# The first feed-forward pair's down projection with tokens on the partitions, and its result turned by VectorE's 32x32 transposes

## The chip, the core and the metric

The kernel runs on one core of a Trainium2 chip. The metric is the device time of one execution in microseconds; before the change it is 1059.04 us, the median of three runs (1058.98 to 1059.52). On the core, TensorE multiplies matrices, VectorE, ScalarE and GpSimd do the elementwise work, and SP (SyncE) issues most of the DMAs. Each engine works through its own list of instructions in order.

## The reference

Attention with a block-causal mask over four batches of eight heads (576 positions, head size 64) gives 2304 tokens of 512 numbers. Two feed-forward pairs follow, each 512 to 2048 to 512, with different activations. All is float32.

```python
scores = scale * np.matmul(q, k.transpose(0, 1, 3, 2))
scores = np.where(block_i >= block_j, scores, -1e9)     # blocks of 64 positions
attn = softmax(scores)
x = (attn @ v).transpose(0, 2, 1, 3).reshape(2304, 512)
h = x @ moe_w_in                                        # first pair
y = np.maximum(0.01 * h, h) @ moe_w_out
h = y @ moe2_w_in                                       # second pair
g = np.where(h >= 1, h, np.where(h <= -1, 0, (h + 1) ** 2 / 4))
out = g @ moe2_w_out
```

## The kernel before

**Precision.** TensorE multiplies float32r, so most operands are split in a high and a low part, and a product is three matmuls: high by high, high by low, low by high. The names end in h and l: xh, xl; gh, gl; yh, yl; a weight's two parts lie in one tile (w1i, w1o, w2i, w2o). `three` (L536) is that triple.

**Stages.** The tokens go through the first pair in nine blocks j of 256, and the 2048 inner features in sixteen slices f of 128. `up1(j, f)` makes h with the features on the partitions (twelve matmuls), ScalarE makes g of it (L542), and g is split in gh and gl. `down1(j, f)` adds the slice's part of y: w1o stationary, g moving, 256 columns at a time, four groups e of 128 output features with three matmuls each. So y comes out with the output features on the partitions, two groups e in one PSUM bank, and two banks hold the four groups of a block. After f = 15, VectorE and ScalarE copy the four groups to SBUF (ysb, L575) and SP writes them to a DRAM tensor, ydram (L576). Between `up1(j, f)` and `down1(j, f)` stand one other `up1` in blocks 0 to 5 and three from block 6 on.

**Around it.** The attention of batch 0 comes first, beside the conversion of the first pair's weights; the heads of batches 1 to 3 are laid between the `up1` and `down1` of blocks 0 to 5. Batches 2 and 3 turn their probabilities by VectorE's 32x32 transposes (L316), DMAs to a DRAM tensor z (L321, pieces of 128 bytes) and DMAs back (pT, L341). One h bank serves `up1` while attention goes on. In blocks 6 and 7 the second pair's weights are staged through DRAM (L148, L151), in block 8 they are loaded (w, L155) and split (w2i, w2o). `load_y` reads ydram back as yh and yl, 512 tokens at a time. The second pair (`up2`, `down2`, from 650 us on) multiplies hh out of w2i and y, does cl, sq, gg, ggh, ggl on VectorE and ScalarE, and has g stationary and w2o moving with 512 columns: the tokens come out on the partitions.

**The order.** Up to block 5, `arrange` (L812) plans the order of each engine's list by a list schedule with prices from `span` (L761). From block 6 on the framework orders by the order in which the code was written and by what is free. Tiles of one tag share a ring of slots; a new tile waits until the slot's last reader is done. The g, gh and gl tiles come from the pool `two` up to block 5 (three slots each) and from the pool `bp` after (two, three and three). The second pair's pool `gp` (cl, sq, gg and so on) lies where the first pair's `two` and `one` pools lay.

Of the kernel before, what the change touches and what calls it, by code (L numbers as in the profile page):

```python
# [9 lines left out]
F32 = mybir.dt.float32  # L10
# [40 lines left out]
def attention_moe_moe(ctx: ExitStack, tc: tile.TileContext, qkv, w1, w2, out, B, H, S, D):  # L51
    nc = tc.nc
    NT, DM = out.shape
# [23 lines left out]

    ident = const.tile([P, P], F32, name="ident")
    make_identity(nc, ident)
    ydram = dram.tile([P, KC, NT], F32, name="ydram")  # L80
    wdram = dram.tile([KF, P, 1024], F32, name="wdram")

    def psum(tag, name):
# [474 lines left out]

    def down1(j, f):
        if f == 0:  # L560
            for e in range(0, KC, 2):
                y = psum("y", f"y{j}_{e}")
                for k in range(2):
                    yt[e + k] = y[:, k * NB:(k + 1) * NB]
        g = gt.pop((j, f))
        for e in range(KC):
            es = slice(e * P, (e + 1) * P)

            start, stop = f == 0 and e % 2 == 0, f == KF - 1 and e % 2 == 1
            wh, wl = W[1, "o", f]  # L570
            three(yt[e], wh[:, es], wl[:, es], *g, start, stop)
        if f == KF - 1:
            for e in range(KC):
                ysb = two_p.tile([P, 320], F32, tag="sc", name=f"ysb{j}_{e}", bufs=C["sc"])[:, :NB]
                copy(nc, pick("yevE", e), ysb, yt[e])  # L575
                nc.sync.dma_start(ydram[:, e, j * NB:(j + 1) * NB], ysb)  # L576

    blocks = [(t0, min(512, NT - t0)) for t0 in range(0, NT, 512)]
    ys = {}
# [1 line left out]
    def load_y(j):  # L581
        t0, n = blocks[j]
        y32 = yp.tile([P, KC, 512], F32, tag="y32", name=f"y32_{j}", bufs=1)
        nc.sync.dma_start(y32[:, :, :n], ydram[:, :, t0:t0 + n])
# [71 lines left out]
    for j in range(NBLK):  # L656
        final = j == NBLK - 1
        due_now(j)
        if j == due[-1]:
            arrange(tc)  # L660
            actx.close()
            gpool = (ctx.enter_context(tc.tile_pool(name="bp", bufs=2, reuse_waits="tile")), C["gB"], C["ghB"])
            sctx = ExitStack()
            sg = sctx.enter_context(tc.tile_pool(name="sg", bufs=C["sg"], reuse_waits="tile"))
        if final:
# [95 lines left out]
def span(ins, e, outs, srcs):  # L761
# [12 lines left out]
    w = max(n(x) for x in outs[:1] + srcs[:1]) if outs else 1  # L774
    if op == "DMACopy":
        kb = outs[0][2][0][1] * n(outs[0]) / 256
        small, spread = (x[0][0].name.startswith("z") for x in (outs, srcs))
        return 1350 + kb * 4.8 + 600 * spread, 520, kb * (7.6 if small else 6 if spread else 3.3)
    if e == "PE":
        if srcs[0][3] == F32 and not ins.is_transpose:  # L780
            return w / 0.6 + 165, w / 0.6 + 95, 0
        step = w / 2.4 + (17 if w >= 512 else 13)
        wide = n(srcs[1]) > 64 and w < 256 and not ins.is_transpose
# [219 lines left out]
```

## Time and profile before

| | |
|---|---|
| median of three runs | 1059.04 us |
| the profiled execution's own time | 1055.33 us |
| its span, first to last instruction | 1053.4 us |
| TensorE busy | 1009.1 us (96%) |
| VectorE busy | 716.8 us (68%) |
| ScalarE busy | 466.1 us (44%) |
| GpSimd busy | 226.4 us (21%) |
| granted TensorE clock, mean | 0.992 of full speed |

A share is a mean over the whole span and hides that stages have different limits, so the table by stretch of time is the one to read. A matmul's shown duration is longer than its pitch, since matmuls are pipelined: the pitch is read from the starts, or from a count of them over a stretch without a gap. What is after the arrow in a row (`<-ACT g L542`) is the instruction whose end let a waiting one go. SP's rows are issues of DMAs; how long a DMA takes to land is another row.

### The profile page before, as it was taken

How to read it: one execution, taken by the hardware profiler on the slowest of the kernel's cores; microseconds unless marked ns; L12 is line 12 of the kernel's file. 1: busy time of each engine (PE TensorE's matmuls, PEld its weight loads, DVE VectorE, ACT ScalarE, POOL GpSimd, SP SyncE). 2: the span in 40 equal slices, each digit the busy share in tenths (PEclk: the TensorE clock that was granted, in tenths of full speed). 3: DMA queues.
4: the chain of work that ended last, by engine and by line, in shares of the span. 5: the costliest groups of instructions: out<-in, count | busy, mean ns of one | idle time of the engine just before them, and what ended most of it. 6: DMA issues, size and time to landing. Idle time of an engine off the chain costs nothing. (4 is left out here: it accounts for less than half of the span.)

```text
span 1053.4 us, 18317 instructions
## 1 busy us (share of the span) xinstructions
PE 1009.1 (96%) x6382; PEld 896.7 (85%) x6382; DVE 716.8 (68%) x1866; ACT 466.1 (44%) x1163; POOL 226.4 (21%) x297
## 2 busy tenths in 40 slices
PE   8899889999999999898999899999999999999998
PEld 6568879998998989898999898888888888888887
DVE  7999999997888878887687778435333533433343
ACT  5676557684655545544444321223322422322233
POOL 4552022252332544534010145000000000000000
PEclk9999999999999999999999899999999999999999
DMA  9655112226677766665788765000100100000010
GB/s 351 218 161 176 45 53 73 59 68 145 146 160 160 153 156 135 148 148 114 236 291 292 239 232 177 1 1 15 66 1 1 60 1 0 20 21 1 1 40 21
DMA packets 161292, 115.50 MB, mean 110 GB/s; under 512 B 110768, under 2 KB 134320, under 8 KB 161200
## 3 DMA queue, kind: packets, MB, share of 16 engines
q1 hardware_dynamic: 158608, 109.62, 36.7%
q10 hardware_dynamic: 2592, 4.72, 1.2%
q8 instruction: 50, 0.82, 0.3%
q14 instruction: 42, 0.34, 0.1%
HBM read 83.62 MB, written 30.67 MB: 109 GB/s over the span
## 5 line engine op out<-in xcount | busy, mean ns | idle before, releaser
L537 PE MATMUL h<-xh,w1i 128*128 128x256 f32 x576 | 168.3, 292 | 14.9 <-ACT g L542 11.3
L538 PE MATMUL h<-xl,w1i 128*128 128x256 f32 x576 | 165.5, 288 | 4.7 <-DVE xl L38 4.2
L538 PE MATMUL y<-gl,w1o 128*128 128x256 f32 x576 | 163.9, 287 | 4.8 <-DVE gl L38 4.3
L539 PE MATMUL h<-xh,w1i 128*128 128x256 f32 x576 | 164.6, 286 | 0.0
L537 PE MATMUL y<-gh,w1o 128*128 128x256 f32 x576 | 160.6, 287 | 1.9 <-DVE gh L32 1.4
L539 PE MATMUL y<-gh,w1o 128*128 128x256 f32 x576 | 162.2, 284 | 0.0
L716 ACT ACTIVATE sq<-cl,half 128x512 f32<-128x512 f32 (+1 forms) x80 | 54.3, 679 | 198.6 <-DVE cl L715 198.5
L715 DVE TENSOR_SCALAR cl<-hh 128x512 f32<-128x512 f32 (+1 forms) x80 | 51.0, 637 | 128.8 <-PE hh L539 127.8
L537 PEld LDWEIGHTS h<-xh,w1i 128*128 128x128 f32 x576 | 110.4, 192 | 20.3 <-ACT g L542 15.7
L300 ACT ACTIVATE p<-s,nm 64x64 f32<-64x64 f32 (+2 forms) x192 | 91.2, 478 | 71.5 <-DVE nm L286 31.3
L537 PE MATMUL hh<-yh,w2i 128*128 128x512 f32 (+1 forms) x320 | 118.0, 369 | 0.0
L538 PE MATMUL hh<-yl,w2i 128*128 128x512 f32 (+1 forms) x320 | 118.0, 369 | 0.0
L539 PE MATMUL hh<-yh,w2i 128*128 128x512 f32 (+1 forms) x320 | 117.8, 368 | 0.0
L538 PEld LDWEIGHTS h<-xl,w1i 128*128 128x128 f32 x576 | 110.5, 192 | 6.5 <-DVE xl L38 5.5
L538 PEld LDWEIGHTS y<-gl,w1o 128*128 128x128 f32 x576 | 109.7, 190 | 7.1 <-DVE gl L38 6.9
L731 PE MATMUL o<-w2o,ggl 128*128 128x512 f32 x288 | 114.0, 396 | 0.0
L732 PE MATMUL o<-w2o,ggh 128*128 128x512 f32 x288 | 113.9, 396 | 0.0
L539 PEld LDWEIGHTS h<-xh,w1i 128*128 128x128 f32 x576 | 110.3, 192 | 0.1
L537 PEld LDWEIGHTS y<-gh,w1o 128*128 128x128 f32 x576 | 108.1, 191 | 2.7 <-DVE gh L32 1.7
L539 PEld LDWEIGHTS y<-gh,w1o 128*128 128x128 f32 x576 | 109.7, 190 | 0.2
L717 DVE TENSOR_TENSOR gg<-hh,sq 128x512 f32<-128x512 f32 (+1 forms) x80 | 51.0, 638 | 52.2 <-ACT sq L716 51.9
L286 DVE TENSOR_REDUCE nm<-s 128x1 f32<-128x288 f32 (+2 forms) x192 | 80.7, 426 | 7.7 <-PE s L277 4.4
(112 smaller groups left out, 2088.5 us busy)
## 6 DMA issues: line engine op xcount, KB each, us to landing
wr<-in_w_dram SPq DMA_DIRECT2D x64, 512.0 KB, 5.7
wdram<-wt SPq DMA_DIRECT2D x32, 256.0 KB, 4.3
w<-wdram SPq DMA_DIRECT2D x16, 512.0 KB, 3.9
rq<-in_qkv_dram SPq DMA_DIRECT2D x24, 288.0 KB, 3.0
rk<-in_qkv_dram SPq DMA_DIRECT2D x24, 288.0 KB, 2.9
pT1l<-z SPq DMA_DIRECT2D x16, 384.0 KB, 4.0
ydram<-ysb SPq DMA_DIRECT2D x36, 128.0 KB, 2.3
z<-p SPq DMA_DIRECT2D x64, 72.0 KB, 2.4
```

What stands on the lines that cost most here:

```text
L286: mark["D"] = nc.vector.tensor_reduce(nm[:n, j:j + 1], s[:n, :kw], axis=AX.X, op=ALU.max, negate=True)
L300: mark["A"] = nc.scalar.activation(o, s, AF.Exp, bias=nm[:n, 0:1], scale=es, accum_out=sm[:n, j:j + 1])
L537: nc.tensor.matmul(ps_ap, wh, xh, start=first, stop=False)
L538: nc.tensor.matmul(ps_ap, wh, xl, start=False, stop=False)
L539: nc.tensor.matmul(ps_ap, wl, xh, start=False, stop=last)
L715: nc.vector.tensor_scalar(cl[:, :n], h[:, :n], -1.0, 1.0, op0=ALU.max, op1=ALU.min)
L716: nc.scalar.activation(sq[:, :n], cl[:, :n], AF.Square, bias=half[:, 0:1], scale=0.5)
L717: nc.vector.tensor_tensor(g32[:, :n], h[:, :n], sq[:, :n], op=ALU.max)
L731: nc.tensor.matmul(ot[m], gl[:, ms], wh, start=False, stop=False)
L732: nc.tensor.matmul(ot[m], gh[:, ms], wl, start=False, stop=f == KF - 1)
```

## The change

`down1` now has a slice of gh or gl stationary (128 tokens) and w1o's 512 columns moving, as `down2` has. A block's y are two banks, one for each 128 tokens, with the tokens on the partitions. For each f there are two matmuls with gh for each half (w1o high, w1o low) and then the two with gl. After f = 15 VectorE transposes each bank out of PSUM into an SBUF tile yx (two slots), 32x32 block by block, and four DMAs for each half write the blocks, in pieces of 32 tokens, to ydram, which is now laid out as 512 features by 2304 tokens; `load_y` reads it so. ScalarE has no part of this any more. The pool `bp` is gone: g, gh and gl stay in `two`. The planner's prices change for TensorE transposes, for DMAs issued elsewhere than by SP and for writes to ydram; the settings get `'yx': 2`.

```diff
-            for e in range(0, KC, 2):
-                y = psum("y", f"y{j}_{e}")
-                for k in range(2):
-                    yt[e + k] = y[:, k * NB:(k + 1) * NB]
-        g = gt.pop((j, f))
-        for e in range(KC):
-            es = slice(e * P, (e + 1) * P)
-
-            start, stop = f == 0 and e % 2 == 0, f == KF - 1 and e % 2 == 1
-            wh, wl = W[1, "o", f]
-            three(yt[e], wh[:, es], wl[:, es], *g, start, stop)
+            for m in range(NB // P):
+                yt[m] = psum("y", f"y{j}_{m}")
+        gh, gl = gt.pop((j, f))
+        wh, wl = W[1, "o", f]
+        parts = [slice(m * P, (m + 1) * P) for m in range(NB // P)]
+        for m, ms in enumerate(parts):
+            nc.tensor.matmul(yt[m], gh[:, ms], wh, start=f == 0, stop=False)
+            nc.tensor.matmul(yt[m], gh[:, ms], wl, start=False, stop=False)
+        for m, ms in enumerate(parts):
+            nc.tensor.matmul(yt[m], gl[:, ms], wh, start=False, stop=f == KF - 1)
         if f == KF - 1:
-            for e in range(KC):
-                ysb = two_p.tile([P, 320], F32, tag="sc", name=f"ysb{j}_{e}", bufs=C["sc"])[:, :NB]
-                copy(nc, pick("yevE", e), ysb, yt[e])
-                nc.sync.dma_start(ydram[:, e, j * NB:(j + 1) * NB], ysb)
+            for m in range(NB // P):
+                t0 = j * NB + m * P
+                yx = two_p.tile([P, DM], F32, tag="yx", name=f"yx{j}_{m}", bufs=C["yx"])
+                nc.vector.transpose(out=yx, in_=yt[m])
+                for a in range(0, P, 32):
+                    nc.sync.dma_start(
+                        ydram[:, t0 + a:t0 + a + 32].rearrange("(k c) t -> c k t", c=32),
+                        yx[a:a + 32].rearrange("c (k t) -> c k t", t=32),
+                    )
...
-            gpool = (ctx.enter_context(tc.tile_pool(name="bp", bufs=2, reuse_waits="tile")), C["gB"], C["ghB"])
...
-        small, spread = (x[0][0].name.startswith("z") for x in (outs, srcs))
-        return 1350 + kb * 4.8 + 600 * spread, 520, kb * (7.6 if small else 6 if spread else 3.3)
+        small, spread = (x[0][0].name.startswith(("z", "yd")) for x in (outs, srcs))
+        return 1350 + kb * 4.8 + 600 * spread, 520 if e == "SP" else 390, kb * (7.6 if small else 6 if spread else 3.3)
...
+        if ins.is_transpose:
+            return w / 2.4 + 172, 109 if outs[0][2][0][1] > 64 else 172, 0
```

TensorE's list at block 7, the whole of `down1(7, 11)`; y7_0 and y7_2 are the two banks before. Before:

```order
L537 MATMUL y7_0_8837<-gh7_11_9146,w1o11_1567 128x256
L538 MATMUL y7_0_8837<-gl7_11_9147,w1o11_1567 128x256
L539 MATMUL y7_0_8837<-gh7_11_9146,w1o11_1567 128x256
L537 MATMUL y7_0_8837<-gh7_11_9146,w1o11_1567 128x256
L538 MATMUL y7_0_8837<-gl7_11_9147,w1o11_1567 128x256
L539 MATMUL y7_0_8837<-gh7_11_9146,w1o11_1567 128x256
L537 MATMUL y7_2_8838<-gh7_11_9146,w1o11_1567 128x256
L538 MATMUL y7_2_8838<-gl7_11_9147,w1o11_1567 128x256
L539 MATMUL y7_2_8838<-gh7_11_9146,w1o11_1567 128x256
L537 MATMUL y7_2_8838<-gh7_11_9146,w1o11_1567 128x256
L538 MATMUL y7_2_8838<-gl7_11_9147,w1o11_1567 128x256
L539 MATMUL y7_2_8838<-gh7_11_9146,w1o11_1567 128x256
```

And now:

```order
L567 MATMUL y7_0_8162<-w1o11_1531,gh7_11_8423 128x512
L568 MATMUL y7_0_8162<-w1o11_1531,gh7_11_8423 128x512
L567 MATMUL y7_1_8163<-w1o11_1531,gh7_11_8423 128x512
L568 MATMUL y7_1_8163<-w1o11_1531,gh7_11_8423 128x512
L570 MATMUL y7_0_8162<-w1o11_1531,gl7_11_8424 128x512
L570 MATMUL y7_1_8163<-w1o11_1531,gl7_11_8424 128x512
```

Twelve became six with twice the columns, and gl, which was read second, is read fifth.

SP's list where block 3's y is written, among the writes of z and the reads of pT of heads 23 to 25. Before:

```order
L321 DMA z24_5638<-p24_4_5817 32x18x32 x4
L321 DMA z25_5889<-p25_0_5839 32x2x32 x2
L241 DMA rq26_5995<-in_qkv_dram 128x576
L321 DMA z25_5889<-p25_1_6010 32x6x32
L576 DMA ydram_71<-ysb3_0_5960 128x256
```

And now:

```order
L321 DMA z24_5284<-p24_4_5445 32x18x32 x4
L321 DMA z25_5511<-p25_0_5467 32x2x32 x2
L577 DMA ydram_71<-yx3_0_5576 32x16x32 x4
L577 DMA ydram_71<-yx3_1_5582 32x16x32 x4
L247 DMA rk26_5615<-in_qkv_dram 128x576
L255 DMA rv26_5619<-in_qkv_dram 128x320
L341 DMA pT1l8_1845<-z24_5284 64x256
L341 DMA pT1l8_1845<-z24_5284 128x3x256
L341 DMA pT1l8_1845<-z24_5284 128x128
L321 DMA z25_5511<-p25_1_5626 32x6x32 x4
```

Four y writes became eight, and they stand ahead of the next head's loads and of head 24's read.

VectorE's list at the seam to the second pair, with the semaphores that each instruction waits for (DMAHW are DMAs; w2i and w2o are casts and splits of the second pair's weights). Before:

```order
L32 COPY ysb8_0_9983<-y8_0_9431 128x256 [waits PE_49]
L32 COPY ysb8_2_9989<-y8_2_9432 128x256 [waits PE_49]
L32 CAST w2i13_9965<-w2_13_9963 128x512 [waits DMAHW0_49]
L32 CAST w2o13_9968<-w2_13_9963 128x512
L38 TENSOR_TENSOR w2i13_9965<-w2_13_9963,w2i13_9965 128x512 [waits DVE_49]
L739 MEMSET half_10020 128x1 [waits DMAHW2_49,Activation_49]
L715 TENSOR_SCALAR cl0_0_10035<-hh0_0_10022 128x512 [waits DMAHW1_49,DMAHW4_49,PE_49,Activation_49]
L32 CAST w2i14_9997<-w2_14_9995 128x512 [waits DMAHW5_49]
L32 CAST w2o14_10000<-w2_14_9995 128x512
```

And now:

```order
L575 STREAM_TRANSPOSE yx8_1_9122<-y8_1_8661 128x512 [waits PE_49]
L38 TENSOR_TENSOR w2i12_9090<-w2_12_9088,w2i12_9090 128x512 [waits DVE_49]
L32 CAST w2i13_9104<-w2_13_9102 128x512 [waits DMAHW0_49,Pool_49]
L32 CAST w2o13_9107<-w2_13_9102 128x512
L38 TENSOR_TENSOR w2i13_9104<-w2_13_9102,w2i13_9104 128x512 [waits DVE_49]
L742 MEMSET half_9153 128x1
L718 TENSOR_SCALAR cl0_0_9168<-hh0_0_9155 128x512 [waits DMAHW3_49,DMAHW2_49,DMAHW4_49,DMAHW1_49,PE_49]
L32 CAST w2i14_9130<-w2_14_9128 128x512 [waits DMAHW1_49,Pool_49]
L32 CAST w2o14_9133<-w2_14_9128 128x512
L720 TENSOR_TENSOR gg0_0_9170<-hh0_0_9155,sq0_0_9169 128x512 [waits Activation_49]
```

The first `cl` waits for four DMAs instead of two, the writes of yx8_0, whose place in SBUF it takes; and the casts of w2 wait for GpSimd as well as for their load.

## Rows read from the trace of the kernel before

**Rows 1.** The page, part 1: busy us, share of the span, instructions.
```profile
PE 1009.1 (96%) x6382; PEld 896.7 (85%) x6382; DVE 716.8 (68%) x1866; ACT 466.1 (44%) x1163; POOL 226.4 (21%) x297
```

**Rows 2.** Busy time by stretch of the span; columns as in the first line.
```profile
core 0: us, PE busy (x) PEld busy (x) DVE busy (x) ACT busy (x) POOL busy (x), PEclk, DMA share, GB/s
0.00:80.00 80.00, 73.24 (x341) 50.32 (x342) 70.86 (x282) 52.17 (x168) 40.55 (x61) 0.98 0.68 242
80.00:160.00 80.00, 70.33 (x514) 64.28 (x513) 78.31 (x201) 47.69 (x120) 13.49 (x18) 0.98 0.29 94
160.00:228.00 68.00, 66.89 (x543) 64.50 (x542) 62.14 (x221) 50.54 (x154) 22.87 (x29) 1.00 0.23 64
228.00:497.00 269.00, 253.49 (x2000) 245.05 (x1998) 222.62 (x661) 147.42 (x417) 113.61 (x164) 0.99 0.64 142
497.00:650.00 153.00, 145.79 (x1170) 143.66 (x1171) 118.47 (x238) 54.09 (x122) 29.95 (x25) 0.98 0.74 248
650.00:1000.00 350.00, 350.00 (x1523) 285.16 (x1522) 142.85 (x219) 95.86 (x147) 5.97 (x4) 1.00 0.06 19
```

**Rows 3.** The timeline of TensorE in block 8: start us, us, what.
```profile
642.05 0.28 PE L537 MATMUL y<-gh,w1o 128*128 128x256 f32 x1
...
644.92 0.38 PE L537 MATMUL y<-gh,w1o 128*128 128x256 f32 x1
```

**Rows 4.** Busy time in a stretch of the second pair, columns as in rows 2.
```profile
680.00:720.00 40.00, 40.00 (x175) 32.56 (x174) 15.22 (x22) 9.63 (x15) 0.00 (x0) 1.00 0.00 0
```

**Rows 5.** TensorE's waits: whole span, then 240 to 440 us, then 120 to 160.
```profile
PE h L537 <- ACT g L542: 11.3, 14, 1.8
PE y L538 <- DVE gl L38: 4.3, 5, 1.2
...
PE h L537 <- ACT g L542: 6.4, 8, 1.6
...
PE y L538 <- DVE gl L38: 1.0, 1, 1.0
```

**Rows 6.** VectorE's groups by shape: out<-in xcount | busy us, mean ns | idle before.
```profile
L715 DVE TENSOR_SCALAR cl<-hh 128x512 f32<-128x512 f32 x64 | 44.2, 691 | 119.4 <-PE hh L539 118.3 <-DMA ydram<-ysb 0.9
L316 DVE STREAM_TRANSPOSE p<-p 128x576 f32<-128x576 f32 x16 | 12.3, 766 | 2.0 <-POOL p L47 1.9
L316 DVE STREAM_TRANSPOSE p<-p 128x448 f32<-128x448 f32 x16 | 10.3, 642 | 4.1 <-POOL p L47 3.5 <-DMA pT1l<-z 0.5
L32 DVE COPY ysb<-y 128x256 f32<-128x256 f32 x18 | 7.3, 413 | 0.6 <-PE y L539 0.5
```

**Rows 7.** The timeline of SP's queue around block 1's y writes.
```profile
244.09 1.84 SPq L576 DMA_DIRECT2D ydram<-ysb  x4
...
248.73 7.19 SPq L321 DMA_DIRECT2D z<-p  x12
```

**Rows 8.** SP's longest waits in 228 to 497 us: us, times, longest.
```profile
SPq L321 <- DVE p L316: 11.6, 14, 1.7
SPq L321 <- DVE nm L286: 4.0, 7, 1.7
```

**Rows 9.** DMA issues of the page: xcount, KB each, median us to landing.
```profile
w<-wdram SPq DMA_DIRECT2D x16, 512.0 KB, 3.9
...
ydram<-ysb SPq DMA_DIRECT2D x36, 128.0 KB, 2.3
z<-p SPq DMA_DIRECT2D x64, 72.0 KB, 2.4
```

**Rows 10.** The timeline at the seam to the second pair.
```profile
649.26 0.28 PE L539 MATMUL y<-gh,w1o 128*128 128x256 f32 x1
...
652.96 0.69 DVE L715 TENSOR_SCALAR cl<-hh 128x512 f32<-128x512 f32 x1 [0.91 <-DMA ydram<-ysb]
...
655.33 0.43 DVE L32 CAST w2i<-w 128x512 fp32r<-128x512 f32 x1 [1.68 <-DMA w<-wdram]
...
660.06 1.09 PE L730 MATMUL o<-w2o,ggh 128*128 128x512 f32 x4
```

More of the change, by code (lines that the diff above doesn't have):

```diff
@@ new lines @@
+C = {'yx': 2, 'WARM': 7, 'DT': [0, 0, 1, 1], 'LAGD': 2, 'VLD': 4, 'WS': 1, 'RS': 2, 'zb': 2, 'dhE': 'PA', 'dlE': 'DD', 'wrE': 'SSSS', 'rdE': 'S', 'PR': '', 'pW': '', 'pS': '', 'p2': '', 'pL': '', 'pG': '', 'lkE': 'D', 'fE': 'A', 'stF': 'A', 'SPLIT': [0, 0, 0, 0], 'WIN': [[0.75, 1.86], [2, 3.86], [3.9, 5.86]], 'PF': [8, 0, 0, 0], 'VF': [8, 0, 0, 0], 'FL': 2, 'LD': 1, 'rcE': 'D', 'fold': 'D', 'evL': 'D', 'ptb': 1, 'PACE': 1, 'LAG0': 1, 'LAG': 3, 'VL0': 2, 'VL': 1, 'YL': 1, 'YL2': 3, 'gB': 2, 'ghB': 3, 'F32S': 6, 'F32V': 6, 'CS': 4, 'CR': 7, 'CN': 12, 'WAHEAD': 5, 'WL': 10, 'cE': 'APPP', 'addE': 'DP', 'hiE': 'DA', 'loE': 'DD', 'evH': 'AAD', 'xeE': 'A', 'norm': 'PPPPP', 'vhiE': 'D', 'vloE': 'P', 'ghE': 'DA', 'glE': 'DD', 'xhE': 'AAPP', 'xlE': 'PDDP', 'B1S': 0.5, 'FILL': 0.96, 'STR': 1.2, 'sc': 4, 'g': 3, 'gh': 3, 'klE': 'D', 'khE': 'P', 'stA': 'PP', 'stC': 'PA', 'yevE': 'DA', 'w2lo': 'DP', 'w2hi': 'DD', 'S0': 'att', 'T0': 'y', 'V0': 'h', 'natt': 5, 'evA': 'A', 'LY': 4, 'LYB': 4, 'yhE': 'AD', 'ylE': 'DD', 'osE': 'AA', 'qhE': 'D', 'sg': 3, 'TS': 1, 'norm_0': 'P', 'xlE_1': 'DPPP', 'evH_0': 'A', 'xhE_1': 'ADPA', 'norm_1': 'ADADA', 'fold_0': 'P', 'qhE_1': 'D', 'glE_0': 'DD', 'evA_1': 'AA', 'klE_2': 'P', 'klE_3': 'P', 'vloE_3': 'P', 'qhE_2': 'A', 'khE_2': 'P', 'vhiE_1': 'P', 'vloE_2': 'P', 'vloE_1': 'P', 'qhE_3': 'A', 'xlE_2': 'PDDP', 'xeE_2': 'AD', 'vhiE_3': 'A', 'norm_2': 'DADPA', 'xeE_1': 'DA', 'xhE_0': 'DDAA', 'xlE_0': 'PDPP', 'evH_1': 'A', 'evA_0': 'AA', 'fold_1': 'P', 'vloE_0': 'D', 'vhiE_0': 'D', 'khE_1': 'P', 'ghE_1': 'DD', 'fE_e': 'AP', 'hiE_e': 'DP', 'loE_e': 'DD', 'dlE_3': 'PD'}
@@ L79, in attention_moe_moe @@
     make_identity(nc, ident)
-    ydram = dram.tile([P, KC, NT], F32, name="ydram")
+    ydram = dram.tile([DM, NT], F32, name="ydram")
     wdram = dram.tile([KF, P, 1024], F32, name="wdram")
@@ L583, in load_y @@
         y32 = yp.tile([P, KC, 512], F32, tag="y32", name=f"y32_{j}", bufs=1)
-        nc.sync.dma_start(y32[:, :, :n], ydram[:, :, t0:t0 + n])
+        nc.sync.dma_start(y32[:, :, :n], ydram.rearrange("(e p) t -> p e t", p=P)[:, :, t0:t0 + n])
         for c in range(KC):
@@ L781, in span @@
             return w / 0.6 + 165, w / 0.6 + 95, 0
+        if ins.is_transpose:
+            return w / 2.4 + 172, 109 if outs[0][2][0][1] > 64 else 172, 0
         step = w / 2.4 + (17 if w >= 512 else 13)
-        wide = n(srcs[1]) > 64 and w < 256 and not ins.is_transpose
+        wide = n(srcs[1]) > 64 and w < 256
         return w / 2.4 + 172, max(step, 109 if wide else 59), 0
```

1 line of the change is left out of this document (removed).

## The prediction

> **What bounds the kernel now.** I read the page first: TensorE is busy 96% of the span [rows 1]. Then the table by stretch [rows 2], because that share is a mean over unlike stages. From 650 us on (the second pair) TensorE is busy 350.00 of 350 us; the change touches nothing there, so whatever moves the end of the first pair moves the end of the kernel. The reader is to see three kinds of stretch before it. In 80 to 160 us (attention of batch 0 beside block 0) VectorE is busy 78.31 of 80 us and TensorE only 70.33: VectorE sets the pace. In 160 to 497 us (attention of the other batches beside blocks 1 to 5) TensorE is at 94 to 98%, VectorE at 83 to 91%. In 497 to 650 us (blocks 6 to 8 alone) TensorE is at 95%. So a shorter `down1` counts in blocks 1 to 8, and not in block 0.
>
> **TensorE's part.** One `down1(j, f)` was twelve matmuls of 256 columns. Back to back, 24 of them go from 642.05 to 644.92 us [rows 3]: 2.87 / 24 = 0.1196 us each, 1.435 us for twelve. Now it is six of 512 columns with a slice of gh or gl stationary and w1o moving. The second pair's `o` matmuls have exactly this form, and a stretch with nothing but 512-column matmuls shows 175 in 40.00 us [rows 4]: 0.2286 us each, 1.371 us for six. The difference is 0.064 us; times 144 it is 9.2 us, times the 128 of blocks 1 to 8 it is **8.2 us saved**. The streamed columns are the same (12 x 256 = 6 x 512); what goes is the part of a pitch that does not depend on the columns, 12 times against 6. Both prices are rows, so I keep them.
> The Trainium skill's page "TensorE: Matmul & The Clock Gate", section "Back-to-back issue gap", gives an isolated gap of N/2.4 + 2.5 ns. By that (an estimate from that page) `down1` would go from 1.310 to 1.295 us, 2 us in 128 of them. The rows have about 13 ns over the streamed columns where the page has 2.5, so the measurement decides.
>
> **The wait for gl.** `down1` needed gl at its second matmul, one pitch after its start; now the gl matmuls are the last two, four pitches (0.91 us) after it. The first fence on the order shows it. TensorE waited for gl 4.3 us in five places, 1.0 of it in block 0, the longest 1.2 [rows 5]. Each of the other four (3.3 us) can lose 0.8 us or all it has, so the bounds are 0 and 2.8 us. What is late next is `up1`: its one h bank is freed by ScalarE's g, for which TensorE waited 11.3 us in 14 places. I take **1.0 us saved**. Those waits grow where less work stands before them: eight in 240 to 440 us [rows 5], times 0.064 us, **0.5 us lost**.
>
> **Taking y out of PSUM.** Before, two copies on VectorE (413 ns) and two on ScalarE per block. Now two 32x32 transposes of 128x512 on VectorE. No row has a transpose out of PSUM. Out of SBUF one takes 642 ns at 448 columns and 766 at 576 [rows 6], so 704 at 512; another VectorE operation of 128x512 out of PSUM takes 691. I take 0.70 us, because both rows agree; the upper end is twice that, should the transpose read PSUM at half rate, the lower 0.69. Per block VectorE gets 2 x 0.70 - 2 x 0.41 = 0.58 us more, ScalarE loses its two. In block 0, where VectorE sets the pace, that is on the path: **0.6 us lost**. In the others the cover is the `up1` work between the last matmul on a y bank and the next block's first: at least twelve matmuls (1.4 us, both transposes end to end), 28 by the order after block 6. If VectorE is late there by one instruction, 0.7 us is lost per block. At the upper price the sum gets 0.7 x 18 = 12.6 us of VectorE work, of which block 0's 1.4 us is on the path for certain.
>
> **The writes to DRAM.** Four DMAs per block become eight, of 128-byte pieces. All are issued by SP, and in 228 to 497 us SP is the queue of the attention as well: the second fence shows eight writes ahead of the loads and reads of the next heads. Four y writes took 1.84 us of SP, twelve z writes (the same 128-byte form) 7.19 us [rows 7], so 0.46 to 0.60 us an issue. Blocks 1 to 4 fall into that stretch: 16 more issues, 7.4 to 9.6 us of SP, middle 8.5. SP had waiting in that stretch that can take it up: 11.6 + 4.0 us in its two longest waits alone [rows 8]. A head takes 269 / 16 = 16.8 us there, and its values stand four tiles behind its read. I take **1.0 us lost**, half of one burst, with the ends 0 and 8.5. ydram's reads keep their 2 KB pieces and cost nothing new.
> The Trainium skill speaks against this edit: "DMA: Bandwidth & Descriptors", section "Rules for kernel authors", wants many small transfers made one large, since under 64 KB most is overhead. Each new write is 64 KB. The rows agree in part: a z write of 72 KB lands in 2.4 us, a y write of 128 KB in 2.3 [rows 9]. By that rule the price is the number of issues, which is the first rival below.
>
> **The seam to the second pair.** The last y matmul starts at 649.26 us, the first `cl` at 652.96 after a wait for a y write, the first `o` at 660.06 [rows 10], 10.8 us behind. `cl` lies in the memory of yx, and the third fence shows it waiting for four writes. The matmul's 0.28, a transpose 0.7, four issues 1.84, landing 2.4: `cl` some 5.2 us behind instead of 3.7. Behind it on VectorE stand the w2 casts of f = 14, whose load SP issues after all eight writes: 0.28 + 0.7 + 3.7, and 3.9 to land [rows 9], so 8.6 us. Before, they waited for the same load and started 6.1 us behind. With two casts at 0.43 and gg at 0.7, gg is there about 10 us behind, ggh 11; TensorE has four hh banks to fill (48 x 0.2286 = 11.0 us) before it needs either. The cover is nearly all used up: **0.7 us lost**, ends 0 and 2. The same fence shows the w2 casts waiting for GpSimd too, since the weight pool hands out other slots now.
>
> **What else moves.** The order up to block 5 is a planner's, and its prices are changed for TensorE transposes and y writes, so attention's steps stand in other places. In 80 to 160 us VectorE has 1.7 us idle that a better order could use; a worse one is a rival. The ring of g keeps three slots in blocks 6 to 8; TensorE had no wait for g there, so nothing.
>
> **Sum.** -8.2 - 1.0 + 0.5 + 0.6 + 1.0 + 0.7 = -6.4 us. The profiled execution has a span of 1053.4 us and a time of 1055.33 us, 3.7 us under the median of the runs, 1059.04; the 1.9 us outside the span stay. I lay the difference on the median: **1052.6 us**.
>
> **Rivals.**
> SP sets the pace of 228 to 497 us (slower). All 16 extra issues land on the path (+8.5), and TensorE's gain in that stretch is worth nothing; left are block 1's 1.0 and blocks 6 to 8's 3.1 us. -4.1 + 8.5 + 0.6 + 0.7 = +5.7, so 1064.7 us. For it: SP issues in long unbroken rows there. Against: its waits [rows 8], and TensorE itself at 94%. It ends slower by over 0.2% once ten of the sixteen issues (about 4.9 us) are on the path. 0.14.
> The attention sets the pace of blocks 1 to 5, through VectorE or ScalarE, and TensorE only waits longer: 48 x 0.064 = 3.1 saved in blocks 6 to 8, 1.3 lost, 1057.2 us. For it: VectorE at 91% in 160 to 228 us. Against: TensorE is at 98% there. 0.10.
> The new order leaves VectorE as idle in 80 to 160 us as it is in 0 to 80 (9.1 us instead of 1.7): 7.4 us onto the sum, 1060.0 us. 0.05.
> That six matmuls do not come out shorter than twelve has no chance of its own, both pitches being rows.
>
> **How the numbers follow.** My forecast has 0.71. 0.2% is 2.1 us, about what a measurement of this kernel tells from no change. Faster is the forecast, 0.71; within 0.2% are the second and third rival, 0.15; slower the first, 0.14. The low end is all 144 `down1` (9.2), all of the gl waits (2.8), block 0's idle time (1.7) and only the 0.6 lost: -13.1, so 1046. The high end takes in the second and third rival: 1061. Left out are the first rival and 0.04 below.
>
> **What would show it.** 864 matmuls of 512 columns at a pitch of 0.229 us and a `down1` of 1.37 us; transposes at 0.70 us; waits for gl near zero; blocks 6 to 8 shorter by about 3 us. Against me: SP without waits in the z stretch and TensorE waiting for v or x; transposes near 1.4 us; a gap on TensorE at the first `o`.

## The result, and the profile after

The changed kernel takes 1047.47 us, the median of four runs (1046.02 to 1052.14), against 1059.17 us for the kernel before on the same chip: a ratio of 0.9897, 95% interval 0.9865 to 0.9928, so 11.7 us less. Its profiled execution took 1046.77 us with a span of 1045.0 us. The forecast was 1052.6 us, 1046 to 1061.

Runs of one kernel lie up to 7 us either side of their median, and one of them 11 us above it, in part by how long TensorE's clock stays at its lower level, so medians carry the comparisons, and a single profile shows where, not how much.

The page's part 1 of the kernel after (busy us, share of the span, instructions), against [rows 1]:

```profile
PE 1004.2 (96%) x5518; PEld 847.8 (81%) x5518; DVE 719.7 (69%) x1866; ACT 459.0 (44%) x1145; POOL 227.1 (22%) x297
```

864 instructions of TensorE are gone and as many weight loads; 1728 matmuls of 256 columns became 864 of 512. By stretch (the columns of [rows 2]):

```profile
80.00:160.00 80.00, 74.23 (x451) 63.33 (x448) 77.43 (x207) 47.41 (x125) 14.56 (x20) 0.96 0.29 81
160.00:228.00 68.00, 65.26 (x439) 56.67 (x437) 62.82 (x222) 49.21 (x149) 23.21 (x28) 1.00 0.23 64
228.00:497.00 269.00, 252.48 (x1608) 224.72 (x1607) 222.43 (x661) 145.22 (x409) 112.37 (x165) 0.99 0.68 144
497.00:650.00 153.00, 148.66 (x905) 131.61 (x905) 122.62 (x236) 51.68 (x115) 31.55 (x22) 0.99 0.81 252
```

In 80 to 160 us TensorE is busy 74.23 us where it was 70.33, beside a VectorE that is no busier than before (77.43 against 78.31). In 228 to 497 us the shares are those of before. The first matmul of the second pair (hh) starts at 640.61 us, against 649.38.

The timeline of TensorE at the last `down1` of block 7 (start us, us, what):

```profile
597.22 0.39 PE L567 MATMUL y<-w1o,gh 128*128 128x512 f32 x1
597.45 0.39 PE L568 MATMUL y<-w1o,gh 128*128 128x512 f32 x1
597.68 0.39 PE L567 MATMUL y<-w1o,gh 128*128 128x512 f32 x1
597.91 0.39 PE L568 MATMUL y<-w1o,gh 128*128 128x512 f32 x1
598.14 0.62 PE L570 MATMUL y<-w1o,gl 128*128 128x512 f32 x2
598.61 0.28 PE L537 MATMUL h<-xh,w1i 128*128 128x256 f32 x1
```

Six matmuls in 598.61 - 597.22 = 1.39 us; forecast 1.37. What counts is the difference to the twelve before, so the rows are better taken as in [rows 3], one `down1` right behind the other, in block 8 (the first matmul of a `down1`, and the first of the third one behind it):

```profile
634.11 0.40 PE L567 MATMUL y<-w1o,gh 128*128 128x512 f32 x1
...
638.31 0.40 PE L567 MATMUL y<-w1o,gh 128*128 128x512 f32 x1
```

Three `down1` in 4.20 us are 1.40 us each, a pitch of 0.233 us where 0.2286 was forecast. Against the 1.435 us of [rows 3] that saves 0.035 us a `down1`, and not 0.064. TensorE's waits (us, times, longest), against [rows 5]:

```profile
PE h L537 <- ACT g L542: 9.6, 11, 2.8
...
PE h L537 <- POOL xh L34: 2.3, 1, 2.3
...
PE y L570 <- DVE gl L38: 1.8, 3, 0.8
PE y L567 <- DVE gh L32: 1.6, 2, 1.3
...
PE y L567 <- DVE yx L575: 1.3, 1, 1.3
```

The waits for gl fell from 4.3 to 1.8 us (2.4 in a second profile of this kernel). A y bank waited once for a transpose, 1.3 us (2.1 in the second profile). The new pieces: the transposes (duration in ns: least, median, most), and the page's row of their DMAs (KB each, us to landing):

```profile
L575 DVE STREAM_TRANSPOSE yx<-y x18: 673/703/717, 152.7 to 642.9; 128x512 f32<-128x512 f32 x18
...
ydram<-yx SPq DMA_DIRECT2D x72, 64.0 KB, 2.2
```

And the seam to the second pair, for [rows 10]:

```profile
640.03 0.73 PE L570 MATMUL y<-w1o,gl 128*128 128x512 f32 x2 [0.62 <-DVE gl L38]
...
646.20 0.68 DVE L718 TENSOR_SCALAR cl<-hh 128x512 f32<-128x512 f32 x1
...
650.55 0.43 DVE L32 CAST w2i<-w 128x512 fp32r<-128x512 f32 x1 [3.67 <-DMA w<-wdram]
...
651.97 0.50 PE L537 MATMUL hh<-yh,w2i 128*128 128x512 f32 x1 [0.29 <-DVE gg L720]
...
653.00 1.09 PE L733 MATMUL o<-w2o,ggh 128*128 128x512 f32 x4
```

The first `o` starts 13 us behind the last y matmuls, 2 us more than before, yet TensorE had hh matmuls up to there and waited 0.29 us. The first `cl` has no idle time before it: it stood behind VectorE's work on w2, not behind the writes. From the first hh to the start of the last matmul it is 400.2 us, before 399.6.

### The profile page after: what moved, and what is told of

The parts are those of the page before. It is cut to its first block, busy times and chain, and to the rows that moved or that the text cites. A ratio compares the mean times of both kernels' runs of the same rounds, so it can differ in the third digit from the quotient of the medians.

```text
span 1045.0 us, 16636 instructions
## 1 busy us (share of the span) xinstructions
PE 1004.2 (96%) x5518; PEld 847.8 (81%) x5518; DVE 719.7 (69%) x1866; ACT 459.0 (44%) x1145; POOL 227.1 (22%) x297
## 5 line engine op out<-in xcount | busy, mean ns | idle before, releaser
L537 PE MATMUL h<-xh,w1i 128*128 128x256 f32 x576 | 167.7, 292 | 11.9 <-ACT g L542 9.6
L567 PE MATMUL y<-w1o,gh 128*128 128x512 f32 x288 | 116.3, 404 | 2.9 <-DVE gh L32 1.6
L568 PE MATMUL y<-w1o,gh 128*128 128x512 f32 x288 | 113.9, 396 | 0.0
L735 PE MATMUL o<-w2o,ggh 128*128 128x512 f32 x288 | 113.9, 396 | 0.0
L570 PE MATMUL y<-w1o,gl 128*128 128x512 f32 x288 | 93.4, 400 | 2.0 <-DVE gl L38 1.8
L542 ACT ACTIVATE g<-h 128x256 f32<-128x256 f32 x144 | 54.1, 378 | 77.1 <-PE h L539 73.9
L733 PE MATMUL o<-w2o,ggh 128*128 128x512 f32 x288 | 86.0, 396 | 0.0
L722 DVE TENSOR_TENSOR ggl<-gg,ggh 128x512 fp32r<-128x512 f32 (+1 forms) x80 | 51.1, 638 | 47.6 <-ACT ggh L721 47.1
```

The costliest lines, as they stand in the source:

```text
L537: nc.tensor.matmul(ps_ap, wh, xh, start=first, stop=False)
L567: nc.tensor.matmul(yt[m], gh[:, ms], wh, start=f == 0, stop=False)
L568: nc.tensor.matmul(yt[m], gh[:, ms], wl, start=False, stop=False)
L570: nc.tensor.matmul(yt[m], gl[:, ms], wh, start=False, stop=f == KF - 1)
L733: nc.tensor.matmul(ot[m], gh[:, ms], wh, start=f == 0, stop=False)
L735: nc.tensor.matmul(ot[m], gh[:, ms], wl, start=False, stop=f == KF - 1)
```

## The experiments

Three parts of the change can be switched on their own: the form (new matmuls, transposes, eight writes), by blocks; the planner's prices; the pool `bp`. Each median below stands beside the kernel before on the same chip, whose medians are 1058.65 to 1058.94 us. What the profiles show of each stands in a table behind the runs.

One thing has to be kept in mind with all of them. The planner makes the order up to block 5 anew whenever the instructions or the prices there change. By the traces, TensorE's and SP's lists up to the last write of x have the same sequence in four pairs: before and no bp, prices alone and old form, changed and new below 6, old form and new from 6 (the names are those of the table). In the runs on gl, on the turning and on ScalarE's queue they differ from the changed kernel's, so those runs hold another order besides their edit.

### The changed kernel again

> The changed kernel once more, nothing edited, as the yardstick for the runs beside it and for a second profile. Every theory: between 1046 and 1052 us, about 11 us under the kernel before. What it tells apart is what belongs to the kernel and what to one execution. If the stretch from the last write of x to the first hh matmul is again near 136 us (before: 142.6) and blocks 1 to 5 again about as long as before, then the gain sits in blocks 6 to 8 (theory A). If these lengths move by 3 us or more with where the granted clock falls, then the place of the gain in one profile is an accident of the clock (theory B).

1047.12 us (1045.34 to 1047.71, four runs), ratio 0.989, 0.9859 to 0.9922. The gain is firm. From the last write of x to the first hh it is 137.6 us (136.1 in the first profile), as theory A has it; the stretch before moved by 2.9 us.

### The form with the old prices

```diff
-        small, spread = (x[0][0].name.startswith(("z", "yd")) for x in (outs, srcs))
-        return 1350 + kb * 4.8 + 600 * spread, 520 if e == "SP" else 390, ...
+        small, spread = (x[0][0].name.startswith("z") for x in (outs, srcs))
+        return 1350 + kb * 4.8 + 600 * spread, 520, ...
-        if ins.is_transpose:
-            return w / 2.4 + 172, 109 if outs[0][2][0][1] > 64 else 172, 0
```

> The changed kernel with the planner's old prices (TensorE transposes, DMAs, ydram), so that only the order up to block 5 differs. Theory A (the first y leaves 2.7 us earlier because the new prices give a better order in the stretch of batch 0): the first transpose of y comes at about 155 us again and the kernel is 2 to 4 us slower than the changed one. Theory B (the order is worth nothing): within 1 us of the changed kernel, first transpose within 1 us of 152.7.

1049.56 us (seven runs), ratio 0.9919, 0.9891 to 0.9947: 2.4 us above the changed kernel's second measurement, with intervals that overlap. The first transpose starts at 154.9 us, in the changed kernel at 152.7 and 153.4. That is theory A, not clear of the spread.

### The prices alone

The kernel before with the three new prices and nothing else (the lines of the diff above, the other way round).

> The kernel before with the planner's new prices and nothing else. Theory C: 2 to 6 us under the kernel before, from a better order in the stretches up to block 5; from the last write of x to the first hh matmul it stays at 142.6 us. Theory B: within 1 us of the kernel before.

1050.10 us (twelve runs), ratio 0.9925, 0.9898 to 0.9951. Some 8.8 us come without one changed matmul, more than either theory had. The term that the prediction put at zero is larger than its whole sum of 6.4.

### The price of TensorE's transposes alone

```diff
+        if ins.is_transpose:
+            return w / 2.4 + 172, 109 if outs[0][2][0][1] > 64 else 172, 0
```

> The kernel before with one of the planner's three new prices alone: a TensorE transpose is booked at 109 ns (172 ns for a narrow one) in place of the matmul's price; the price of ydram's writes and of issues from other queues stay as they were. All three prices together gave 1050.10 us against 1058.94. If the booking of the transposes alone makes the better order: 1049 to 1052 us. If the DMA prices make it: 1057 to 1060. If neither is worth anything and the gain of all three was a lucky order: anything between, and the profile's start to the last x write (510 us before) tells where.

1047.23 us (1042.65 to 1048.88, six runs), ratio 0.9881, 0.9855 to 0.9908: this one line gives as much as the whole change, and more than was expected of it. What moves is only the order. TensorE's groups of h and y in 0 to 497 us, the kernel before, then this one (xcount | busy us, mean ns | idle before):

```profile
L538 PE MATMUL h<-xl,w1i 128*128 128x256 f32 x386 | 110.4, 286 | 1.3 <-DVE xl L38 0.9 <-POOL xl L38 0.4
L538 PE MATMUL y<-gl,w1o 128*128 128x256 f32 x380 | 107.8, 287 | 3.8 <-DVE gl L38 3.4 <-DVE rc L308 0.3
```

```profile
L538 PE MATMUL h<-xl,w1i 128*128 128x256 f32 x392 | 111.2, 284 | 0.4 <-DVE xl L38 0.3
L538 PE MATMUL y<-gl,w1o 128*128 128x256 f32 x384 | 108.5, 285 | 2.1 <-DVE gl L38 2.1
```

By 497 us it has done six and four more triples of 256 columns, which at 0.1196 us a matmul [rows 3] is 10 x 3 x 0.1196 = 3.6 us of work ahead, and its waits for xl and gl are smaller. In 80 to 160 us, where VectorE sets the pace, TensorE is busy 3.0 us more than before:

```profile
80.00:160.00 80.00, 73.33 (x538) 67.58 (x537) 77.03 (x209) 48.01 (x127) 14.68 (x21) 0.96 0.25 82
```

Of these 3.0 us, 1.7 are the lower clock, which lasts 6.8 us in this stretch and 3.4 in the kernel before; 1.3 are work. And the lead doesn't last: counted in the two traces at 0.1196 us a matmul, this kernel is 1.6 us of h and y ahead at 160 us, 0.5 at 300 and 4.2 at 440. So most of the gain doesn't come from where VectorE sets the pace.

Why this price orders better wasn't tried further, nor whether another price would do as well by luck. One row bears on it: in the trace of before five 128-column transposes start at 110.90 us and the next matmul at 111.36, 0.092 us each; the planner booked 0.066 (128 / 2.4 + 13 ns) and now books 0.109, which is not the measured value either.

### The kernel before without the pool bp

```diff
-            gpool = (ctx.enter_context(tc.tile_pool(name="bp", bufs=2, reuse_waits="tile")), C["gB"], C["ghB"])
```

> The kernel before without the pool bp: g, gh and gl keep their three slots in the pool two in blocks 6 to 8. Theory C allows 0 to 4 us less, all of it behind the last write of x: 139 to 142 us from there to the first hh matmul instead of 142.6. Theory B, and the prediction: nothing, since TensorE had no wait for g in those blocks.

1056.87 us (twelve runs), ratio 0.9984, 0.9966 to 1.0002. Some 2 us by the medians; the interval goes from 3.6 us less to no difference. From the last x to the first hh nothing moved (142.7 us, before 142.6), against theory C.

### The old form, all else as in the change

> The old form of down1, its copies and its four writes in all nine blocks, with all the rest of the change: the planner's new prices, g, gh and gl kept in the pool two, ydram as 512 by 2304. If the two mixed kernels and the changed one add up (-14.5, -5.8, -11.7 us against the kernel before), the part that they share is worth -14.5 - 5.8 + 11.7 = -8.6 us. Theory C (the shared part carries most of the gain): 6 to 10 us under the kernel before, the first y copy 2 us earlier. Theory B (the form carries it, by 0.064 us for each down1): within 2 us of the kernel before.

1048.89 us (1043.0 to 1052.35, six runs), ratio 0.9903, 0.9869 to 0.9938. With the new prices the whole new form is worth only 1.4 to 1.8 us more, which isn't clear of the spread. Theory C's 6 to 10 us hold; the first y copy comes 1.1 us earlier, not 2.

### The new form in blocks 6 to 8 alone

```diff
+    def down1(j, f):
+        (down1_new if j >= 6 else down1_old)(j, f)
```

> The new form of down1 with its transposes only in blocks 6, 7 and 8; blocks 0 to 5 have the old twelve matmuls, the copies and four writes. Theory A (the gain sits in blocks 6 to 8): 5 to 7 us under the kernel before. Theory B (each down1 saves the same 0.064 us, as forecast): 48 of 144, so 3 us under it, and up to 1 us more for the waits on gl.

1044.34 us (four runs), ratio 0.9874, 0.983 to 0.9918. Both theories are far off, since this kernel has the new prices too. Against the old form with the same prices, and the same lists up to block 5, it is 4.6 us. And once more:

> The same kernel as e6_new_from_6 once more, with more rounds: the new form of down1 and the transposes in blocks 6 to 8 alone, the old form in blocks 0 to 5. If its 1044.3 us was no draw of the clock: 1043 to 1046 us, 2 to 4 us below the changed kernel's 1047.1. If it was one: 1047 to 1049, as the old form everywhere (1048.9) or the changed kernel.

1043.44 us (1041.94 to 1044.83, five runs), ratio 0.9854, 0.9829 to 0.9879. This is the fastest version found, 15 us under the kernel before, 5.4 under the old form with the same lists, and by the medians some 3 to 4 under the changed one.

### The new form in blocks 0 to 5 alone

```diff
+    def down1(j, f):
+        (down1_new if j < 6 else down1_old)(j, f)
```

> The reverse: new form in blocks 0 to 5, old form in 6 to 8. Theory A: 2 to 4 us under the kernel before (block 0's order, nothing from blocks 1 to 5). Theory B: 80 of the down1 in blocks 1 to 5 save 5.1 us, and with the waits on gl 5 to 7 us under it. The two mixed kernels together should give back the whole gain of about 11 us if the parts add; if both give little, the gain needs both.

1053.03 us (ten runs), ratio 0.9948, 0.9925 to 0.997. The interval lies wholly above that of the changed kernel's second measurement and of the reverse kernel. The changed kernel has the same lists up to block 5 and is 5.6 to 5.9 us faster, so blocks 6 to 8 carry the form's gain. In 0 to 5 the form, with the order that the planner makes for it, costs 4.1 us by the medians (against the old form, all else as in the change). The 5.8 us under the kernel before are in theory B's range, but not for its reason, since the prices alone give 8.8.

### gl second again

Each half's three matmuls in the order gh with w1o high, gl with w1o high, gh with w1o low.

```diff
-            nc.tensor.matmul(yt[m], gh[:, ms], wl, start=False, stop=False)
-        for m, ms in enumerate(parts):
-            nc.tensor.matmul(yt[m], gl[:, ms], wh, start=False, stop=f == KF - 1)
+            nc.tensor.matmul(yt[m], gl[:, ms], wh, start=False, stop=False)
+            nc.tensor.matmul(yt[m], gh[:, ms], wl, start=False, stop=f == KF - 1)
```

> The changed kernel with the matmuls of a half in the old order: gh by w1o high, gl by w1o high, gh by w1o low, so that gl is needed one pitch (0.23 us) after the start of down1 instead of four (0.91). The prediction's step on gl: 1 us slower than the changed kernel, at most 2.8, with TensorE's waits for gl at 4 us or more instead of 1.8. If the late gl does more (it keeps the granted clock up by taking the gaps away), 3 us or more slower.

1058.62 us (twelve runs), ratio 0.9993, 0.9968 to 1.0017: the whole gain is gone. TensorE's waits in its profile (us, times, longest):

```profile
PE y L568 <- DVE gl L38: 4.1, 6, 1.3
PE o L732 <- ACT ggh L720: 3.9, 1, 3.9
PE v L427 <- DVE pT1h L38: 3.3, 2, 1.7
```

The wait for gl is back (4.1 us, against 1.8), and a gap of 3.9 us stands at the seam, where the changed kernel has 0.3. That is 6 us. The first hh to the last matmul takes 405.3 us, 5.1 more than in the changed kernel. The rest is spread over the order, which the planner made anew, and over 34 us at the lower clock before the last x write (14 to 20 in the changed kernel). The wait itself moved by 2.3 us, more than the 1.0 forecast and inside its bounds; how much of the other 9 us comes of it and how much of the order stays open.

### No turning

y copied as it stands, by four copies a block, and written by four DMAs in 1 KB pieces.

```diff
-                nc.vector.transpose(out=yx, in_=yt[m])
-                for a in range(0, P, 32):
-                    nc.sync.dma_start(
...
+                copy(nc, pick("yevE", e), ysb, yt[m][:, k * NB:(k + 1) * NB])
+                nc.sync.dma_start(ydram[e * P:(e + 1) * P, j * NB:(j + 1) * NB], ysb)
```

> The changed kernel without the turning: y stays with tokens on the partitions, is copied out of PSUM by four copies a block as before the change and written by four DMAs a block in 1 KB pieces, so that what lies in ydram is y in another layout and the later numbers are of that; every shape after it is the same. It takes away 2 transposes of some 0.70 us for 4 copies shared by two engines and 4 of 8 writes a block. My sum priced them at +0.6 (block 0) and +1.0 us (SP's queue): 1045 to 1047 us if that is right, against 1047.1 for the changed kernel. If the writes or the transposes are what eats the shorter matmuls' gain in blocks 0 to 5 (some 4 us at full clock): 1042 to 1044.

1044.94 us (1044.36 to 1046.09, five runs), ratio 0.9869, 0.9844 to 0.9893: by the medians transposes and extra writes cost some 2.2 us together. The two intervals leave that uncertain by some 4 us, so no cost isn't excluded, and the order up to block 5 is another one. From the first hh to the last matmul it is 399.6 us again, so 0.6 of that is the seam. The prediction had 0.6 + 1.0 + 0.7 = 2.3 for these; so close an agreement is luck.

### The writes on ScalarE's queue

```diff
-                    nc.sync.dma_start(
+                    nc.scalar.dma_start(
```

> The changed kernel with the eight writes of y a block issued from ScalarE's queue in place of SP's. If SP's burst of 8 issues holds the reads of the probabilities (my term of +1.0 us, bound 8.5): 1046 down to 1039 us. If SP has time for them, as its stretch of 267 us in both traces says: 1047 with a spread of 3, and no shift of the waits on w or pT. If ScalarE's queue is the worse place, because an issue stands behind copies that wait: 1049 to 1052, with longer waits of h on ScalarE's g.

1053.07 us (twelve runs), ratio 0.9944, 0.9923 to 0.9966: 6 us worse, not better. Rows of its profile: the landing of the writes, a wait of TensorE at the seam, and a wait of SP in 228 to 497 us.

```profile
ydram<-yx ACTq DMA_DIRECT2D x72, 64.0 KB, 3.6
...
PE hh L537 <- DVE gg L720: 2.7, 1, 2.7
...
SPq L321 <- DMA ydram<-yx: 5.6, 6, 1.9
```

The writes land in 3.6 us instead of 2.2, the second pair starts with a gap of 2.7 us (404.2 us from the first hh to the end, 4.0 more), and SP's z writes now wait for them. TensorE's waits of h on g, which were to grow, are 8.0 us (9.6). So 4 of the 6 us stand behind the first hh. For the rest the other order can't be told from the queue, but nothing speaks for ScalarE as the place.

### What the profiles show together

One profile each. The columns: the form in blocks 0 to 5 and in 6 to 8; the median; the profiled run; the time from the start to where the last write of x begins (the end of attention), from there to the first hh (blocks 6 to 8), and how long the trace records the clock at its lower level in each of the two, all in us.

| kernel | 0–5 | 6–8 | median | profiled | to last x | to first hh | low clock |
|---|---|---|---|---|---|---|---|
| before | old | old | 1059.0 | 1055.3 | 506.8 | 142.6 | 10.2 / 6.8 |
| no bp | old | old | 1056.9 | 1055.8 | 507.1 | 142.7 | 17.0 / 10.2 |
| prices alone | old | old | 1050.1 | 1061.0 | 513.0 | 142.1 | 27.2 / 6.8 |
| transpose price alone | old | old | 1047.2 | 1047.5 | 500.6 | 140.9 | 13.6 / 3.4 |
| old form, all else | old | old | 1048.9 | 1048.9 | 500.7 | 142.4 | 6.8 / 6.8 |
| new below 6 | new | old | 1053.0 | 1053.8 | 505.6 | 142.5 | 20.4 / 6.8 |
| changed | new | new | 1047.5 | 1046.8 | 504.5 | 136.1 | 20.4 / 0 |
| changed, again | new | new | 1047.1 | 1045.3 | 501.6 | 137.6 | 13.6 / 3.4 |
| old prices | new | new | 1049.6 | 1054.8 | 510.2 | 137.9 | 27.2 / 0 |
| new from 6 | old | new | 1044.3 | 1049.8 | 507.3 | 136.8 | 13.6 / 0 |
| new from 6, again | old | new | 1043.4 | 1043.1 | 501.0 | 136.3 | 13.6 / 0 |

The clock doesn't explain all that differs between runs of one kernel: the two profiles of new from 6 have 13.6 us at the lower level before the last x each, and differ by over 6 us there.

**Blocks 6 to 8.** Six traces with the old form there have 140.9 to 142.7 us, mean 142.2; the five with the new form 136.1 to 137.9, mean 136.9. The three kernels with the new form that the table leaves out (gl second, no turning, ScalarE's queue) have 136.6 to 137.6. So the form gives 5.3 us in 48 `down1`, where 48 x 0.064 = 3.1 was forecast. The medians of the two pairs with the same lists up to block 5 say the same: 4.6 to 5.4, and 5.6 to 5.9 us. More than half of it is the clock. At the end of block 7 all old-form traces have TensorE waiting and then running at the lower level; in the kernel before, the timeline and then the table by stretch (columns of [rows 2]):

```profile
593.14 0.38 PE L537 MATMUL h<-xh,w1i 128*128 128x256 f32 x1 [1.79 <-ACT xh L30]
...
596.42 0.58 PE L538 MATMUL h<-xl,w1i 128*128 128x256 f32 x1 [1.46 <-DVE xl L38]
...
590.00:595.00 5.00, 3.10 (x20) 2.29 (x18) 3.92 (x8) 2.11 (x5) 1.84 (x3) 1.00 0.72 263
595.00:600.00 5.00, 3.58 (x16) 3.58 (x17) 3.64 (x7) 1.23 (x4) 1.00 (x2) 0.57 0.28 77
```

The changed kernel, and then the old form with all else changed, in the same place:

```profile
585.00:590.00 5.00, 3.68 (x15) 2.30 (x14) 3.94 (x8) 1.95 (x5) 0.00 (x0) 1.00 0.89 282
590.00:595.00 5.00, 3.92 (x22) 2.67 (x22) 4.89 (x8) 2.78 (x7) 2.93 (x4) 1.00 0.44 168
595.00:600.00 5.00, 5.00 (x38) 4.74 (x38) 4.88 (x11) 1.36 (x4) 1.40 (x1) 1.00 0.57 156
```

```profile
585.00:590.00 5.00, 1.95 (x9) 1.39 (x8) 3.84 (x7) 2.43 (x7) 0.88 (x1) 0.86 0.47 185
590.00:595.00 5.00, 4.42 (x21) 4.13 (x21) 4.21 (x8) 1.07 (x3) 1.96 (x4) 0.50 0.20 74
```

The granted clock of 0.50 is the lower of the two levels (1.2 GHz); the gaps ahead of it are TensorE's waits for x's next parts. In the changed kernel TensorE is busy 3.68 + 3.92 of 10 us around its own gaps there, and the clock stays at 1.00. Its longest gap there is 1.3 us, in the six old-form traces it is 1.6 to 3.1; that the shorter gaps are what keeps the clock up is argued, not shown. Half of 6.8 us at the lower clock is 3.4 us, half of 3.4 us is 1.7; the old form loses 1.7 to 5.1 us so, the new one nothing in four traces of five. Less that, it is 138.8 against 136.6, so 2.2 us are left. The measured saving of 0.035 us a `down1` makes 1.7 of them, and shorter waits about the rest: TensorE's gaps in this stretch add up to 5.4 us in the mean of the six, 4.6 in the five.

**Blocks 0 to 5.** With the new prices, the new form there makes the median 2.8 to 4.1 us longer (new from 6 to changed, old form to new below 6). Each of these differences alone is within what the medians can miss, but the two pairs agree. In both the order up to block 5 changes with the form, so what they price is the two together. One place where time is lost is the end of block 3. First SP's queue in the changed kernel, then ScalarE's list and TensorE's, then TensorE's row by stretch:

```profile
361.80 5.55 SPq L321 DMA_DIRECT2D z<-p  x10
367.44 0.42 SPq L241 DMA_DIRECT2D rq<-in_qkv_dram  x1
...
370.96 0.68 ACT L43 ACTIVATE qs<-rq 128x576 fp32r<-128x576 f32 x1 [4.00 <-DMA rq<-in_qkv_dram]
372.86 0.36 ACT L542 ACTIVATE g<-h 128x256 f32<-128x256 f32 x1
...
373.27 0.58 PE L537 MATMUL h<-xh,w1i 128*128 128x256 f32 x1 [2.75 <-ACT g L542]
...
370.00:375.00 5.00, 2.25 (x13) 2.05 (x12) 3.72 (x13) 3.74 (x11) 3.30 (x5) 0.83 0.63 119
375.00:380.00 5.00, 5.00 (x31) 4.73 (x31) 3.62 (x11) 0.80 (x2) 1.31 (x2) 0.83 0.81 114
```

And SP, TensorE and the stretches with the old form, all else as changed:

```profile
359.55 5.53 SPq L321 DMA_DIRECT2D z<-p  x10
365.18 0.42 SPq L241 DMA_DIRECT2D rq<-in_qkv_dram  x1
...
370.73 0.39 PE L537 MATMUL h<-xh,w1i 128*128 128x256 f32 x1 [0.91 <-ACT g L542]
...
370.00:375.00 5.00, 4.27 (x35) 4.28 (x36) 4.11 (x15) 3.26 (x10) 2.52 (x4) 1.00 0.73 187
375.00:380.00 5.00, 5.00 (x44) 5.00 (x43) 3.79 (x9) 1.63 (x4) 2.63 (x4) 1.00 0.78 186
```

In both kernels the loads of the next head stand on SP behind ten z writes; with the old form these began 2.2 us earlier. In the changed kernel ScalarE waits 4.00 us for rq at qs, and g, which frees the one h bank, stands behind qs. In the changed kernel block 3's y matmuls are over by then (its first transpose starts at 366.1 us) and TensorE has nothing else: 2.75 us idle, 2.5 in the second profile, and then a stretch at the lower clock. With the old form y matmuls ran on to 369.5 us there, rq was issued at 365.18, the gap is 0.91 us, and the clock stayed at 1.00. The attention's loads pace this place, not TensorE. With the old form the planner also put `qs` behind two other steps of ScalarE, so form and order aren't told apart here.

## Why the prediction was right, and where it was wrong

The sign is as forecast and the median lies in the range, but 5.1 us under the predicted time. That it lies in the range is in part luck: the largest term of the sum came out at about half its size, and what made up for it, the order and the lower clock, wasn't in the sum.

- **Pitches.** `down1` itself was nearly right, 1.39 to 1.40 us for 1.37. But the term is the difference to 1.435, and that is 0.035 us instead of 0.064: the 8.2 us saved in 128 `down1` would be 4.5 even with TensorE as the bound everywhere. The step that failed is taking the new pitch from the second pair (0.2286 us); in `down1` the same form has 0.233. The Trainium skill's isolated gap of N/2.4 + 2.5 ns, on its page "TensorE: Matmul & The Clock Gate", section "Back-to-back issue gap", gives 0.216 us for 512 columns, an estimate from that page; the rows above have 0.233, and the measurement decides.
- **"A shorter `down1` counts in blocks 1 to 8, and not in block 0."** This step failed for blocks 1 to 5. Read from shares of 94 to 98%, TensorE was the bound there. The medians give no gain there under the new order, and rather a loss; with the old prices about 2 us are left for these blocks (7.3 below, less the 5.3 of blocks 6 to 8). The rival "the attention sets the pace of blocks 1 to 5, through VectorE or ScalarE, and TensorE only waits longer" describes what the end of block 3 shows. Its price put the gain there at nothing; a loss, and the lower clock that follows a gap, weren't in it.
- **Blocks 6 to 8.** The gain is there, 5.3 us and not 3.1, but the forecast mechanism makes only 1.7 of it. 3.1 us are the lower clock at the end of block 7, which I hadn't looked for in [rows 2], where it stands as 0.98.
- **gl.** The waits fell by 2.5 us in the trace (1.9 in the second), inside the bounds 0 to 2.8. With gl second again the gain is gone, by more than my term; what of that is the wait, and what the order and the clock, stays open.
- **h waits.** Forecast to grow by 0.5 us, they fell from 11.3 to 9.6, though the longest grew from 1.8 to 2.8.
- **Transposes, SP's burst and the seam.** The duration was right (0.703 for 0.70), and so was the price of the seam (0.6 for 0.7), though `cl` stood behind VectorE's work and not behind the writes. The three terms' sum of 2.3 us stands against 2.2 without the turning, a difference that isn't clear of the spread. SP took up the sixteen issues: from the first z write to the last read of pT it is 267.4 us, before 268.6. So the first rival, SP as the pace, is out. The Trainium skill's advice to make many small transfers one large ("DMA: Bandwidth & Descriptors", "Rules for kernel authors") fits that direction, but no run here prices the writes by themselves.
- **"What else moves": zero for the order.** This is the term that was mis-sized most. The prices alone give 8.8 us, one of them alone 11.4, and I had allowed 1.7 us in the low end. The reason I gave was that VectorE sets the pace in 80 to 160 us and has 1.7 us idle. In that stretch the bound about held: TensorE was busy 3.0 and 3.9 us more there, 1.7 of it lower clock, so 1.3 and 2.2 us of work. But the order counts in all of 0 to 497 us, and with the transposes' price alone most of the lead came up between 300 and 440 us.
- **No effect of bp.** Not settled: 2 us by the medians, 3.6 at most by the interval.

The parts don't add up, so a single share for each can't be given:

| medians, us | old form | new form |
|---|---|---|
| old prices, no bp | 1056.9 | 1049.6 |
| new prices, no bp | 1048.9 | 1047.1 |

With the old prices the form gives 7.3 us, close to the forecast of 6.4; with the new ones 1.8. That both take away waits and low-clock stretches at the same places, so that whichever comes first gets them, would explain it, but no run shows it. The 7.3 agrees with the forecast by luck, since 5.3 of it sit in blocks 6 to 8 and 3.1 of those are the clock. The forecast left out what a better order gives besides (2.5 us by this path) and the pool (1.9, with zero not excluded); 7.3 + 2.5 + 1.9 is the result.

What stays open: why the price of the transposes orders so much better, and how much of the loss in blocks 0 to 5 is the clock. In the table above the four traces with the new prices and the old form there (not counting the profile at 1061.0 us) have 6.8 to 13.6 us at the lower clock, the three with the new form 13.6 to 20.4; half of the difference of means (18.1 - 11.9) is 3.1 us, which is the size of the loss, from one profile each. With the profile at 1061.0 us counted in, it is 1.6.

## What to carry to other kernels

A change that touches a planner's prices is two changes: time the prices alone before giving the gain to the code. A saving that is a small difference of two prices should have both read in the place itself: the new form's price was 2% too low, and that took 45% of the saving. A step that makes TensorE's work shorter pays where nothing else paces the stretch, so try it by stage; here the version with the new form in blocks 6 to 8 alone beat the full change. And look behind each gap of TensorE for what the granted clock does next, since that can cost more than the gap.

## What was not expected of the hardware

- Gaps of 1.3 to 4.4 us on TensorE are often followed by 3.4 to 10.2 us at the lower of the two clock levels. In the kernel before, 24 matmuls of 256 columns run there from 597.01 to 602.13 us, 0.213 us each, against 0.1196 at the full level. Not every gap brings one.
- A 32x32 transpose of 128x512 out of PSUM takes 0.703 us, between the 642 ns (448 columns) and 766 ns (576) that [rows 6] have out of SBUF: no extra cost of PSUM shows.
- Matmuls of one form have a pitch of 0.2286 us in the second pair [rows 4] and 0.233 in `down1`, both without gaps at the full clock; why isn't known.
- The same 64 KB writes land in 2.2 us (the median) when SP issues them and in 3.6 from ScalarE's queue.
